# Splitting one block's weights early and turning two blocks on TensorE in an attention and expert kernel

## The chip, the cores and the metric

The program runs on one NeuronCore of a Trainium2 chip. The metric is the device time of one execution in microseconds (us); lower is better. The engines are named as in the profile: PE (TensorE matmuls; PEld its weight loads), DVE (VectorE), ACT (ScalarE), POOL (GpSimd) and SP (SyncE, which issues DMAs here). Each runs its own list of instructions in order and waits on semaphores of the others.

## What is computed

The kernel does a linear attention for 8 batches of 8 heads, 576 positions and 64 dimensions, and feeds each position's 512 values to one of 8 experts.

```python
q_s = exp(q - max(q)); q_s /= sum(q_s) + 1e-9        # over the 64 dimensions
k_s = exp(k - max(k)); k_s /= sum(k_s) + 1e-9        # over the 576 positions
kv  = einsum('bhsd,bhse->bhde', k_s, v)
x   = einsum('bhsd,bhde->bhse', q_s, kv)             # to (batch, position, 512)
logits = x @ w_gate; local_gate = sigmoid(x @ w_local)
for each position: e = argmax(logits), or the expert of the position before where local_gate >= 0.5
    h   = max(x @ w1[e], 0)                          # 512 -> 1024
    out = softmax(logits)[e] * (h @ w2[e])           # 1024 -> 512
```

## The kernel before

The first 200 us or so make the attention and write its rows to DRAM. The positions are then sorted by expert into blocks of 128 rows of one expert, numbered from 0; the tenth block is block 9 (`NP`, `NA` are 9). Blocks 0 to 8 are made from the first two of four row tiles while the attention of the rest still runs; their work stands in a list written out by hand, `ORDER`, in which a name such as `F1.8.0` is a task, its block and its half. `SWAP` names the tasks that run on their other engine (`alt` in `add`). From block 9 on a function `block(b)` writes the code of each block, and a nest of branches ends where no block is left.

The steps of a block are these; f counts the eight pieces of 128 columns of the hidden layer, 0 to 3 in half 0 and 4 to 7 in half 1:

- `G` gathers the block's rows (POOL's indirect DMA), `Px` scales them, `Ph` and `Pl` make a high and a low fp16 part (`x2`). The rows then have to be turned into `xT`: by a transposing DMA on SP (`D`, L880), or by eight PE transposes of 128x128 into the one PSUM tile `pt` (`T`, L874) and a DVE copy (`Tc`, L877).
- `F1.b.g` is the first product of a half (L903, L906; 48 matmuls), `Ar` and `Al` its ReLU as high and low part (ACT L911, DVE L915), `F2.b.g` the second product (L926; 12 matmuls), `Gv` the scaling of the result (ACT L929, which needs the share gathered by `Gp`) and `Pt` the scatter of the rows to the output (POOL L933).
- `RN.b.k` renews the weights where the block is the first of an expert, behind a branch on the flag in `info`: ACT cuts the high part (L190) and DVE the low part (L955) of four pieces. RN.b.0 holds w1's pieces 0 to 3, RN.b.1 its pieces 4 to 7, both out of the staging tile s1; RN.b.2 and RN.b.3 hold w2's out of s2. F1.b.0 needs RN.b.0, F1.b.1 needs RN.b.1.
- `s1.b` and `s2.b` (`fetch`, L998) load the next expert's w1 or w2 (2 MB each) into the staging tiles on SP, with a condition that skips the transfer; they wait until the tile has been cut. In `block(b)` these loads go in four quarters of 512 KB.
- In `hidden` PE uses 64 or 128 columns. From block 9 on PE reads a word of `info` for that (L838, once a block) and branches on it (L889, in both halves), over the code of the other form.
- `Sd.1` stores the shares of the second two tiles (SP); `Gp.9` gathers from them.

`Plan.emit` holds each list to its dependences; engines otherwise follow the written order. DMAs on SP are issued in order, and one that waits holds back those behind it.

Of the kernel before, what the change touches and what calls it, by code (L numbers as in the profile page):

```python
# [18 lines left out]
B, H, S, D = 8, 8, 576, 64  # L19
# [12 lines left out]
NA = 9  # L32
NB = NBM - NA
NP = NA
# [19 lines left out]
class Plan:  # L54
# [7 lines left out]
    def add(self, name, eng, fn, after=(), takes=(), uses=(), order=(), alt=None):  # L62


        eng = alt if name in self.swap else eng
        before = list(order) + list(uses)
        for r, _ in takes:
            if r in self.chained:
                before += [self.head[r]] if r in self.head else []
                self.head[r] = name  # L70
        self.tasks[name] = (eng, fn, list(after), list(takes), before, alt)
        for u in takes:
            self.taker[u] = name
        for u in set(uses) | set(takes):
            self.users.setdefault(u, []).append(name)
# [29 lines left out]


SWAP = """
Ph.0 Ph.11 Ph.2 Ph.3 Ph.4 Ph.6 Ph.9 Pl.10 Pl.11 Pl.6 Pl.8 Px.0 Px.10 Px.4 Px.5 Px.6 Px.9 Wh.15 ex.1.2 ex.3.0 ex.3.2 gs.0.0 gs.0.1 gs.0.2 gs.1.0 gs.1.1
gs.2.0 gs.2.1 gs.2.2 gs.3.0 gs.3.2 norm.3 norm.5 norm.6 put.0 put.2 put.3 put.4 put.6 put.7 qs.2.4 qs.3.6 qs.3.7 ro.0.0 ro.0.2 ro.0.3 ro.0.5 ro.0.7
ro.0.8 ro.1.3 ro.1.7 ro.2.0 ro.2.1 ro.2.2 ro.2.4 ro.2.6 ro.3.0 ro.3.4 ro.3.6 sub.6.1 vc.0.0 vc.0.1 vc.1.0 vc.2.0 vc.3.0 vc.4.0 vc.4.1 vc.5.0 xc.0.0  # L110
xc.0.2 xc.3.5 xc.3.8
# [35 lines left out]
ro.3.4 Ar.6.0 Al.6.0 ro.3.3 F2.5.1 ro.3.5 Sa.1 ro.2.0 Gv.5 RN.7.0 s2.5 RN.6.2 F1.6.1 Ar.6.1 ro.2.2 RN.7.1 RN.6.3 F2.6.0 F1.7.0 bo.3 D.8  # L147
Al.6.1 ro.3.6 s2.6 F2.6.1 ro.3.1 s1.7 RN.8.0 ro.2.1 Gv.6 Ar.7.0 RN.7.3 RN.7.2 bo.0 ro.3.2 bm.3 ro.2.7 Al.7.0 bm.1 bm.2 bm.0 bx.p0 bx
Sb.1 F1.7.1 Pt.5 Ar.7.1 Sc.1 Al.7.1 F2.7.0 F1.8.0 F2.7.1 s2.7 G.9 RN.8.2 Px.9 Ph.9 G.10 G.11 Pt.6 RN.8.1 s1.8 RN.8.3 s2.8
Px.10 Pl.9 Ar.8.0 Al.8.0 Gv.7 Px.11 F1.8.1 T.9 Tc.9 RN.9.1 Ar.8.1 Ph.10 Pt.7 Pl.10 D.10 G.12 F2.8.0 Gp.8 RN.9.0 Ph.11 Sd.1 Pl.11 Gp.9  # L150
Al.8.1 s1.9 D.11
"""


# [1 line left out]
def moe_kernel(ctx, tc, q, k, v, w_gate, w_local, w1, w2, out, dbg=None):  # L156
# [23 lines left out]
    def at(pair, b):  # L180

        return pair[0][:, b] if b < NA else pair[1][:, b - NA]
# [687 lines left out]
    def turn(b):  # L870

        for c in range(4):
            for i in range(2):
                nc.tensor.transpose(pt[0][:, i, c, :], x2[b % 2][:, i, P * c:P * c + P], id16)  # L874

    def turn_copy(b):
        nc.vector.tensor_copy(out=xT[b % 4], in_=pt[0])  # L877
# [5 lines left out]
    def ffn1(b, g):  # L883
        if b < NA:
            hidden(b, g, P)
            return
        if g == 0:
            few[0] = word(at(info, b)[:, 5:6], 1, [ET.PE])
        with tc.If(few[0] == 1) as cmp:  # L889
            hidden(b, g, P // 2)  # L890
        with cmp.Else():
            hidden(b, g, P)
# [77 lines left out]
    def renew(b, pieces):  # L970
        with tc.If(fst[b] == 1):  # L971
            for i in pieces:
                cut_hi(i, nc.scalar)
                cut_lo(i, nc.vector)
# [6 lines left out]
    def fetch(b, i, parts=None):  # L981

        if b >= NBM - 1:
            return
        w_ = at(info, b)
        cond, e = w_[:, 4:5], w_[:, 1:2]
        if NX0 <= b < NA:
            cond, e = w_[:, 2:3] if b == NX0 else w_[:, 0:1], w_[:, 3:4]
        if b not in due:
            due[b] = word(cond, 1, [ET.SP]), word(e, NE - 1, [ET.SP])  # L990
        cond, e = due[b]
        for n in ((None,) if parts is None else parts):
            s_, src = ((W["s1"], w1_src), (W["s2"], w2_src))[i - 1]
            s_, src = s_[:], src(bass.ds(e, 1))
            if n is not None:
                at_ = (slice(None), slice(None), slice(256 * n, 256 * n + 256)) if i == 1 else (slice(None), slice(2 * n, 2 * n + 2))
                s_, src = s_[at_], src[at_]
            nc.sync.dma_start(out=s_, in_=src, cond=(cond == 1), cond_hint=False)  # L998
# [4 lines left out]
    add, split = pl.add, pl.split  # L1003
    plan.append(pl)
    PE, DVE, ACT, POOL, SP = "PE", "DVE", "ACT", "Pool", "SP"
# [88 lines left out]
    for b in range(NP + 4):  # L1094
        add(("G", b), POOL, gather, after=[("ax",) if b < NA else ("bx",)] + [("xs", t, u) for t in range(2 if b < NA else NTILE) for u in range(3)],
            order=[("ow",)], takes=[("xg", b)])
        if b <= NP:
            add(("Gp", b), POOL, gather_share, after=[("ax",) if b < NA else ("bx",)] + [("Sd", t) for t in range(1 if b < NA else 2)],
                order=[("ow",)], takes=[("pb", b)])
        if b >= NP + 3:  # L1100
            continue
        add(("Px", b), POOL, prep_x, alt=DVE, after=[("G", b)], uses=[("xg", b)], takes=[("xn", b)])
        add(("Ph", b), ACT, prep_hi, alt=DVE, after=[("Px", b)], uses=[("xn", b)], takes=[("x2", b)])
        add(("Pl", b), DVE, prep_lo, alt=POOL, after=[("Ph", b)], uses=[("xn", b), ("x2", b)])
        if b in (0, NA):
            add(("T", b), PE, turn, after=[("Pl", b)], takes=[("pst", b)], uses=[("x2", b)])
            add(("Tc", b), DVE, turn_copy, after=[("T", b)], uses=[("pst", b)], takes=[("xT", b)])
        else:
            add(("D", b), SP, turn_dma, after=[("Pl", b)], uses=[("x2", b)], takes=[("xT", b)])
        if b > NP:  # L1110
            continue
        if b > 0:
            for i in range(2 if b == NP else 4):
                src = [("F1", b - 1, 0), ("F1", b - 1, 1), ("F2", b - 1, 0), ("F2", b - 1, 1)][i]
                add(("RN", b, i), ACT, renew4, after=[src, ("aj",) if b < NA else ("bj",)], order=[("s1" if i < 2 else "s2", b - 1)])
            add(("s1", b), SP, lambda b: fetch(b, 1), after=[("RN", b, 0), ("RN", b, 1)] + ([("bj",)] if b >= NX0 else []))
        else:
            add(("s1", b), SP, lambda b: fetch(b, 1), after=[("Wl", i) for i in range(8)] + [("aj",)], order=[("W", 3)])
        if b == NP:
            continue  # L1120
        add(("s2", b), SP, lambda b: fetch(b, 2),
            after=([("RN", b, 2), ("RN", b, 3)] if b else [("Wl", i) for i in range(8, 16)] + [("aj",)]) + ([("bj",)] if b >= NX0 else []))
        for g in range(2):
            wp_ = [("Wl", 4 * g + i) for i in range(4)] if b == 0 else [("RN", b, g)]
            add(("F1", b, g), PE, ffn1, after=[("Tc" if b in (0, NA) else "D", b)] + wp_, order=[("ow",)] + ([("F2", b - 1, g)] if b else [("F1", 0, 0)] * g)
                + ([("F1", b, 0)] if g else []), takes=[("psh", (b, g))], uses=[("xT", b)])
            add(("Ar", b, g), ACT, act_hi, after=[("F1", b, g)], uses=[("psh", (b, g))] + ([("hh", b)] if g else []), takes=[] if g else [("hh", b)])
            add(("Al", b, g), DVE, act_lo, after=[("Ar", b, g)], uses=[("psh", (b, g)), ("hh", b)])
            if b == NP - 1 and g:
                continue  # L1130
            wp_ = [("Wl", 8 + 4 * g + i) for i in range(4)] if b == 0 else [("RN", b, 2 + g)]
            add(("F2", b, g), PE, ffn2, after=[("Al", b, g)] + wp_, order=[("F1", b, 1)] if g == 0 else [("F1", b + 1, 0)],
                takes=[] if g else [("psy", b)], uses=[("hh", b)] + ([("psy", b)] if g else []))
        if b < NP - 1:
            add(("Gv", b), ACT, give, after=[("F2", b, 1), ("Gp", b)], uses=[("psy", b), ("pb", b)], takes=[("y", b)])
            add(("Pt", b), POOL, put, after=[("Gv", b)], uses=[("y", b)])
# [11 lines left out]
    def act(b, g):  # L1148
        act_hi(b, g)
        act_lo(b, g)  # L1150
# [5 lines left out]
    def block(b):  # L1156


        if b + AHEAD < NBM:
            gather(b + AHEAD)  # L1160
        prep_a(b + 3)
        if b + 1 < NBM:
            gather_share(b + 1)
            if b + 1 not in fst:
                flag(b + 1)
        ffn1(b, 0)
        act(b, 0)
        renew(b, FROM[b][0])
        fetch(b, 2, (0, 1) if b == NP else (1,))
        next_(b, (0, 1))  # L1170
        fetch(b + 1, 1, (0,))
        ffn2(b - 1, 1)
        ffn1(b, 1)
        give(b - 1)
        put(b - 1)
        renew(b, FROM[b][1])
        fetch(b, 2, (2,))
        next_(b, (2, 3))
        fetch(b + 1, 1, (1,))
# [64 lines left out]
```

## Time and profile before

| | before |
|---|---|
| median of 3 runs | 551.49 us (549.43 to 553.74) |
| profiled execution, its own time | 551.45 us |
| its span, first to last instruction | 549.7 us |
| PE busy | 493.6 us (90% of the span) |
| DVE, ACT, POOL busy | 276.2, 220.7, 258.1 us |
| mean granted clock of PE | 0.969 |

Times in the trace are counted from the span's start. A "busy" time of PE is modelled, so what counts are its gaps and their releasers: the instruction whose semaphore came last. "issue" stands for a wait with no releaser in the profile. The granted clock is a share of 2.4 GHz: 1.00 is that level, 0.50 is 1.2 GHz. A queue's "q" behind an engine's name (PEldq, SPq) marks instructions of its sequencer: loads of words, branches, issues of DMAs.

### The profile page before, as it was taken

The numbers are of one execution on the slowest core, as the hardware profiler recorded it, in microseconds if no ns is written. First come the engines' busy times: TensorE is split into PE (matmuls) and PEld (weight loads), VectorE is DVE, ScalarE is ACT, GpSimd is POOL, SyncE is SP. The second block draws the span as 40 slices with busy tenths as digits, with TensorE's granted clock in tenths as the row PEclk, the third lists the DMA queues.
The fourth block names the chain that finished last, engine by engine and source line by source line (L and its number), as shares of the span: only waits on it lengthen the run. The fifth ranks groups of instructions, "written<-read, shape, count | busy, mean of one in ns | idle before, by whom it ended". The sixth has DMA issues, their size and how long they took to land. (4 is left out here: it accounts for less than half of the span.)

```text
span 549.7 us, 19358 instructions
## 1 busy us (share of the span) xinstructions
PE 493.6 (90%) x7298; PEld 366.2 (67%) x7298; DVE 276.2 (50%) x501; ACT 220.7 (40%) x388; POOL 258.1 (47%) x284
## 2 busy tenths in 40 slices
PE   1657896767999999988999999999999999999994
PEld 0546775556776767666666777767677767767762
DVE  6889798897754672473128323822562122222221
ACT  1446587896321333343138223622642122222221
POOL 3666786356725340485425425424534324424431
PEclk9998797996999999989999999999999999999998
DMA  8999799487341449459538844872695233342342
GB/s 312 375 382 311 258 341 390 154 320 229 94 100 64 125 146 327 152 166 268 125 84 209 260 80 121 271 160 81 158 292 109 77 83 84 85 83 74 96 73 63
DMA packets 84351, 98.70 MB, mean 180 GB/s; under 512 B 46959, under 2 KB 61295, under 8 KB 84208
## 3 DMA queue, kind: packets, MB, share of 16 engines
q1 hardware_dynamic: 76560, 74.66, 48.0%
q0 software_dynamic: 7648, 22.20, 12.7%
q8 instruction: 82, 1.34, 1.0%
q14 instruction: 61, 0.50, 0.4%
HBM read 207.28 MB, written 20.89 MB: 415 GB/s over the span
## 5 line engine op out<-in xcount | busy, mean ns | idle before, releaser
L903 PE MATMUL ph<-xT,w1h 128*128 128x128 f16 (+1 forms) x2432 | 181.0, 218 | 0.5 <-issue 0.5
L903 PEld LDWEIGHTS <-w1h 128*128 128x128 f16 x2432 | 145.4, 98 | 0.7 <-issue 0.6
L915 DVE SCALAR_TENSOR_TENSOR lo<-ph,hi 128x512 f16<-128x512 f32 x76 | 52.3, 688 | 138.7 <-ACTq L971 130.9
L933 POOL DMA_INDIRECT out<-y,sidx x38 | 40.1, 1056 | 173.3 <-ACTq L971 145.4
L906 PE MATMUL ph<-xT,w1l 128*128 128x128 f16 (+1 forms) x1216 | 115.8, 218 | 5.4 <-issue 2.8
L911 ACT ACTIVATE hi<-ph 128x512 f16<-128x512 f32 x76 | 45.2, 595 | 181.5 <-PE ph L903 124.3
L906 PEld LDWEIGHTS <-w1l 128*128 128x128 f16 x1216 | 82.1, 98 | 23.5 <-issue 4.0
L926 PEld LDWEIGHTS <-hi 128*128 128x128 f16 x608 | 56.2, 98 | 54.4 <-issue 0.2
L926 PE MATMUL py<-w2h,hi 128*128 128x512 f16 x184 | 70.0, 381 | 0.0
L926 PE MATMUL py<-w2l,hi 128*128 128x512 f16 x184 | 69.8, 380 | 0.0
L926 PE MATMUL py<-w2h,lo 128*128 128x512 f16 x184 | 69.7, 379 | 0.0
L867 DVE SCALAR_TENSOR_TENSOR x<-xn,x 128x512 f16<-128x512 f32 x37 | 31.6, 853 | 69.1 <-ACT x L190 65.2
L844 POOL DMA_INDIRECT xg<-xrows,gidx x42 | 46.5, 1106 | 23.8 <-DVE tz L679 12.1
L926 PEld LDWEIGHTS <-lo 128*128 128x128 f16 x304 | 29.8, 98 | 36.0 <-issue 0.3
L926 PE MATMUL pi<-w2h,hi 128*128 128x512 f16 x120 | 45.5, 379 | 0.0
L926 PE MATMUL pi<-w2l,hi 128*128 128x512 f16 x120 | 45.5, 379 | 0.0
L926 PE MATMUL pi<-w2h,lo 128*128 128x512 f16 x120 | 45.5, 379 | 0.0
L850 POOL DMA_INDIRECT pb<-shares,gidx x39 | 41.5, 1065 | 8.3 <-issue 8.2
L431 POOL TENSOR_TENSOR qs<-qt,qm 128x512 f32<-128x512 f32 x33 | 35.3, 1082 | 18.9 <-PE pq L440 17.1
L855 POOL TENSOR_TENSOR xn<-xg 128x512 f32<-128x512 f32 x35 | 37.1, 1060 | 10.9 <-DMA xg<-xrows,gidx 5.0
L322 DVE TENSOR_REDUCE KM<-KT 128x128 f32<-128x1152 f32 x16 | 34.6, 2172 | 4.3 <-DMA KT<-in_k 4.3
L455 PE MATMUL px<-R,qe 64*64 64x74 f32 x864 | 23.2, 249 | 12.3 <-ACT xt L190 6.5
(219 smaller groups left out, 585.0 us busy)
## 6 DMA issues: line engine op xcount, KB each, us to landing
s<-in_moe_w SPq DMA_DIRECT2D x233, 512.0 KB
s<-in_moe_w SPq DMA_DIRECT2D x19, 2048.0 KB
xrows<-xt SPq DMA_DIRECT2D x12, 888.0 KB
KT<-in_k SPq DMA_DIRECT2D x16, 576.0 KB
VT<-in_v SPq DMA_DIRECT2D x16, 576.0 KB
qt<-in_q SPq DMA_DIRECT2D x8, 640.0 KB
qt<-in_q SPq DMA_DIRECT2D x8, 512.0 KB
s<-in_moe_w SPq DMA_DIRECT2D x4, 1024.0 KB
```

The costliest lines, as they stand in the source:

```text
L322: nc.vector.tensor_reduce(out=KM[b % 2][:, 2 * u:2 * u + 2], in_=KT[b % NKT][:, u:KG:2].rearrange("p g c d -> p g d c"), axis=AX.X, op=ALU ...
L431: on("qs", t, c).tensor_tensor(out=qs[t, c].rearrange("p (g x) d -> p g x d", x=2), in0=qt[t, u][:, :, i, :].rearrange("p (x g) d -> p g x ...
L844: nc.gpsimd.indirect_dma_start(out=xg[b % AHEAD], out_offset=None, in_=src, in_offset=bass.IndirectOffsetOnAxis(ap=i_[:, j_:j_ + 1], axis=0))
L850: nc.gpsimd.indirect_dma_start(out=pb[b % NPB], out_offset=None, in_=src, in_offset=bass.IndirectOffsetOnAxis(ap=i_[:, j_:j_ + 1], axis=0))
L855: eng.tensor_tensor(out=xn[b % 2].rearrange("p (g x d) -> p g x d", g=4, x=2), in0=xg[b % AHEAD].rearrange("p (g x) -> p g x", g=4)[:, :, ...
L867: nc.vector.scalar_tensor_tensor(out=x2[b % 2][:, 1, :], in0=xn[b % 2], scalar=XS, in1=x2[b % 2][:, 0, :], op0=ALU.mult, op1=ALU.subtract)
L903: nc.tensor.matmul(ph_[:, f, 0:n], W["w1h"][:, c, fs], xT_[:, i, c, 0:n], start=False, stop=(c == 3 and i == 1))
L906: nc.tensor.matmul(ph_[:, f, 0:n], W["w1l"][:, c, fs], xT_[:, 0, c, 0:n], start=(c == 0), stop=False)
L911: nc.scalar.activation(hi[b % 2][:, 4 * g:4 * g + 4, :], phs[g], AF.Relu)
L915: nc.vector.scalar_tensor_tensor(out=lo[b % 2][:, gs_, :], in0=phs[g], scalar=0.0, in1=hi[b % 2][:, gs_, :], op0=ALU.max, op1=ALU.subtract)
L926: nc.tensor.matmul(result(b), h_[:, f, :], w_[:, f, :], start=(f == 0 and i == 0), stop=(f == 7 and i == 2))
L933: nc.gpsimd.indirect_dma_start(out=outr, out_offset=bass.IndirectOffsetOnAxis(ap=i_[:, j_:j_ + 1], axis=0), in_=ys[b % 2], in_offset=None, ...
```

## The change

The change reorders the end of `ORDER`, from the tenth block's weights on, and touches the planner and `block`:

- RN.9.0 stands right behind Al.8.0, ahead of Gv.7 and of F1.8.1 (it stood last among block 9's cuts, behind Ar.8.1 and Ph.10).
- Blocks 10 and 11 (the eleventh and twelfth) are turned by PE as block 9 is: T.10 and Tc.10 in `ORDER`, block 11's turn in `block(9)`. Their transposing DMAs D.10 and D.11 are gone.
- Pl.10 and Pl.11 leave `SWAP`: they run on DVE, no longer as two instructions each on POOL.
- The load s1.9 is issued as s1.9.0 and s1.9.1, two quarters each, behind RN.9.0 and behind RN.9.1; it was one DMA of 2 MB behind both.

```diff
-Ph.0 Ph.11 Ph.2 Ph.3 Ph.4 Ph.6 Ph.9 Pl.10 Pl.11 Pl.6 Pl.8 Px.0 ...
+Ph.0 Ph.11 Ph.2 Ph.3 Ph.4 Ph.6 Ph.9 Pl.6 Pl.8 Px.0 ...
...
-Px.10 Pl.9 Ar.8.0 Al.8.0 Gv.7 Px.11 F1.8.1 T.9 Tc.9 RN.9.1 Ar.8.1 Ph.10 Pt.7 Pl.10 D.10 G.12 F2.8.0 Gp.8 RN.9.0 Ph.11 Sd.1 Pl.11 Gp.9
-Al.8.1 s1.9 D.11
+Px.10 Pl.9 Ar.8.0 Al.8.0 RN.9.0 Gv.7 Px.11 Ph.10 Pl.10 F1.8.1 T.9 RN.9.1 Tc.9 Sd.1 s1.9.0 s1.9.1 G.12 Ar.8.1 Al.8.1 F2.8.0 T.10 Tc.10 Pt.7 Ph.11 Pl.11
+Gp.8 Gp.9
...
-        if b in (0, NA):
+        if b == NP + 2:
+            continue
+        if b in (0, NP, NP + 1):
             add(("T", b), PE, turn, after=[("Pl", b)], takes=[("pst", b)], uses=[("x2", b)])
...
+            if b == NP:
+                for i in range(2):
+                    add(("s1", b, i), SP, lambda b, i: fetch(b, 1, (2 * i, 2 * i + 1)), after=[("RN", b, i), ("bj",)])
+                continue
...
         ffn1(b, 0)
+        if b == NP:
+            turn(b + 2)
         act(b, 0)
+        if b == NP:
+            turn_copy(b + 2)
         renew(b, FROM[b][0])
```

On PE, between the end of F2.8.0 and the start of F1.9.0, there stands before:

```order
L926 LDWEIGHTS lo_1975
L926 MATMUL py_1966<-w2h,lo_1975 128x512
L838 TENSOR_LOAD info_78
L889 COMPARE_AND_BRANCH
L906 LDWEIGHTS w1l
L906 MATMUL ph_1979<-xT_1958,w1l 128x64
```

and with the change, where the last of T.10's eight transposes are the first rows (x_1955 is block 10's x2, pt_1965 the one PSUM tile for transposes):

```order
L874 LDWEIGHTS x_1955
L874 MATMUL pt_1965<-id_67,x_1955 128x128
L838 TENSOR_LOAD info_78
L889 COMPARE_AND_BRANCH
L906 LDWEIGHTS w1l
L906 MATMUL ph_1979<-xT_1958,w1l 128x64
```

The word's load and the branch, which followed F2.8.0 directly, now follow T.10, whose first transpose has to wait for Pl.10 and for Tc.9. The eight transposes of T.11 stand in the same way between F1.9.0 and F2.8.1.

On DVE, from Al.8.0 to Al.8.1, there stands before (x4 are the four cuts of an RN, first RN.9.1, then RN.9.0; xT_1958 is block 9's, L194 is Ph.11):

```order
L915 SCALAR_TENSOR_TENSOR lo_1975<-ph_1979,hi_1973 128x512
L877 COPY xT_1958<-pt_1965 128x1024
L838 TENSOR_LOAD info_78
L971 COMPARE_AND_BRANCH
L955 SCALAR_TENSOR_TENSOR w1l<-s_1934,w1h 128x4x128 x4
L971 UNCONDITIONAL_BRANCH x2
L971 COMPARE_AND_BRANCH
L955 SCALAR_TENSOR_TENSOR w1l<-s_1934,w1h 128x4x128 x4
L971 UNCONDITIONAL_BRANCH x2
L194 TENSOR_SCALAR x_1956<-xn_1954 128x512
L915 SCALAR_TENSOR_TENSOR lo_1975<-ph_1980,hi_1973 128x512
```

and with the change (the first x4 is RN.9.0, the second RN.9.1, the L867 row is Pl.10, xT_1959 is block 10's):

```order
L838 TENSOR_LOAD info_78
L971 COMPARE_AND_BRANCH
L955 SCALAR_TENSOR_TENSOR w1l<-s_1934,w1h 128x4x128 x4
L971 UNCONDITIONAL_BRANCH x2
L867 SCALAR_TENSOR_TENSOR x_1955<-xn_1953,x_1955 128x512
L971 COMPARE_AND_BRANCH
L955 SCALAR_TENSOR_TENSOR w1l<-s_1934,w1h 128x4x128 x4
L971 UNCONDITIONAL_BRANCH x2
L877 COPY xT_1958<-pt_1965 128x1024
L915 SCALAR_TENSOR_TENSOR lo_1975<-ph_1980,hi_1973 128x512
L889 UNCONDITIONAL_BRANCH
L877 COPY xT_1959<-pt_1965 128x1024
```

Tc.9, which came before all eight cuts, comes behind them, and Pl.10 stands between the two fours.

On SP, the issues behind the load s2.8 stand before as:

```order
L880 DMA_TRANSPOSE xT_1959<-x_1955 128x8x128
L583 DMA shares<-pr 128x2x9
L838 TENSOR_LOAD info_78 x2
L998 REGISTER_ALU x2
L998 ISA
L998 DMA s_1934<-in_moe_w 128x4x1024
L889 UNCONDITIONAL_BRANCH
L880 DMA_TRANSPOSE xT_1960<-x_1956 128x8x128
```

and with the change as:

```order
L583 DMA shares<-pr 128x2x9
L971 UNCONDITIONAL_BRANCH
L838 TENSOR_LOAD info_78 x2
L998 REGISTER_ALU x2
L998 ISA
L998 DMA s_1934<-in_moe_w 128x4x256
L998 ISA
L998 REGISTER_ALU
L998 ISA
L998 DMA s_1934<-in_moe_w 128x4x256
```

Two more quarters like the last follow. The two transposing DMAs around the share store and the load are gone, and the store is first.

## Rows read from the trace of the kernel before

**Rows 1.** Page: busy us (share of the span), instructions.
```profile
PE 493.6 (90%) x7298; PEld 366.2 (67%) x7298; DVE 276.2 (50%) x501; ACT 220.7 (40%) x388; POOL 258.1 (47%) x284
```

**Rows 2.** Stretches: length, then PE, PEld, DVE, ACT, POOL busy, clock, DMA share, GB/s.
```profile
235.07:237.68 2.61, 0.00 (x1) 0.00 (x1) 2.61 (x4) 0.93 (x2) 2.37 (x3) 1.00 0.00 0
...
238.90:242.30 3.40, 3.40 (x32) 3.09 (x30) 1.47 (x3) 0.37 (x1) 3.29 (x3) 0.50 0.77 148
242.30:255.30 13.00, 13.00 (x132) 8.59 (x129) 7.80 (x12) 6.77 (x13) 8.43 (x8) 1.00 1.07 240
255.30:256.77 1.47, 0.00 (x1) 0.00 (x1) 0.00 (x0) 0.99 (x2) 1.31 (x2) 1.00 1.08 398
...
262.22:262.71 0.49, 0.00 (x0) 0.00 (x0) 0.00 (x0) 0.00 (x0) 0.35 (x1) 1.00 0.14 42
262.71:542.40 279.69, 279.69 (x3252) 201.57 (x3252) 91.08 (x129) 92.95 (x156) 111.82 (x106) 1.00 0.52 129
```

**Rows 3.** Waits of PE from 205 us on: us in total, times, longest.
```profile
PE ph L906 <- DVE w1l L955: 2.6, 1, 2.6
```

**Rows 4.** Stretches as in rows 2: F1.8.1; F2.7.1 and F1.8.1; F1.9.0 and F2.8.1.
```profile
229.19:231.87 2.68, 2.68 (x49) 2.68 (x48) 0.00 (x0) 1.94 (x4) 1.01 (x1) 1.00 0.03 9
...
226.60:231.87 5.27, 5.27 (x63) 3.84 (x61) 1.33 (x3) 2.54 (x5) 2.05 (x2) 1.00 0.05 16
237.68:244.60 6.92, 6.92 (x60) 5.29 (x61) 4.73 (x9) 2.67 (x5) 6.04 (x6) 0.75 0.75 167
```

**Rows 5.** ACT in order of time: start us, us, instruction, idle before and its releaser.
```profile
226.80 0.60 ACT L911 ACTIVATE hi<-ph 128x512 f16<-128x512 f32 x1 [5.62 <-PE ph L903]
229.39 0.69 ACT L929 ACTIVATE y<-py,pb 128x512 f32<-128x512 f32 x1 [1.99 <-PE py L926]
230.30 1.15 ACT L190 ACTIVATE w1h<-s 128x512 f16<-128x512 f32 x2 [0.22 <-ACT y L929]
...
233.82 2.18 ACT L190 ACTIVATE w1h<-s 128x512 f16<-128x512 f32 x4
```

**Rows 6.** DVE in order of time; then the eight cuts by line (ns min/median/max).
```profile
232.52 0.69 DVE L877 COPY xT<-pt 128x1024 f16<-128x1024 f16 x1 [4.40 <-PE pt L874]
233.16 6.28 DVE L955 SCALAR_TENSOR_TENSOR w1l<-s,w1h 128x512 f16<-128x512 f32 x8
...
L955 DVE SCALAR_TENSOR_TENSOR w1l<-s,w1h x8: 676/682/1634, 233.2 to 238.8; 128x512 f16<-128x512 f32 x8
```

**Rows 7.** POOL in order of time: the two instructions of Pl.10.
```profile
234.01 1.80 POOL L864 TENSOR_SCALAR xn<-xn 128x512 f32<-128x512 f32 x1 [2.63 <-ACT x L190]
235.89 1.19 POOL L865 TENSOR_TENSOR x<-xn,x 128x512 f16<-128x512 f32 x1
```

**Rows 8.** PE's branches at L889: count, ns min/median/max, first and last start.
```profile
L889 PEldq COMPARE_BRANCH  x1: 4476/4476/4476, 252.2 to 252.2; - x1
...
L889 PEldq COMPARE_BRANCH  x1: 2902/2902/2902, 259.8 to 259.8; - x1
...
L889 PEldq COMPARE_BRANCH  x59: 63/210/1117, 265.1 to 536.6; - x59
```

**Rows 9.** DMA queues from 242.3 to 254.2 us: packets, MB, share of 16 engines.
```profile
q1 hardware_dynamic: 1608, 2.42, 90.6%
...
q14 instruction: 1, 0.01, 0.2%
```

**Rows 10.** SP in order of time: the w1 load (one DMA) and D.11.
```profile
240.41 0.38 SPq L998 DMA_DIRECT2D s<-in_moe_w  x1
243.08 4.06 SPq L880 DMA_TRANSPOSE xT<-x  x1
```

**Rows 11.** PE in order of time at T.9; then PE's word loads by line (ns).
```profile
231.87 0.61 PE L874 MATMUL pt<-id,x 128*128 128x128 f16 x8
232.32 0.38 PE L926 MATMUL py<-w2h,hi 128*128 128x512 f16 x1
...
L838 PEldq TENSOR_LOAD <-info x7: 299/313/774, 232.1 to 299.4; - x7
```

More of the change, by code (lines that the diff above doesn't have):

```diff
@@ L107 @@
 SWAP = """
-Ph.0 Ph.11 Ph.2 Ph.3 Ph.4 Ph.6 Ph.9 Pl.10 Pl.11 Pl.6 Pl.8 Px.0 Px.10 Px.4 Px.5 Px.6 Px.9 Wh.15 ex.1.2 ex.3.0 ex.3.2 gs.0.0 gs.0.1 gs.0.2 gs.1.0 gs.1.1
+Ph.0 Ph.11 Ph.2 Ph.3 Ph.4 Ph.6 Ph.9 Pl.6 Pl.8 Px.0 Px.10 Px.4 Px.5 Px.6 Px.9 Wh.15 ex.1.2 ex.3.0 ex.3.2 gs.0.0 gs.0.1 gs.0.2 gs.1.0 gs.1.1
 gs.2.0 gs.2.1 gs.2.2 gs.3.0 gs.3.2 norm.3 norm.5 norm.6 put.0 put.2 put.3 put.4 put.6 put.7 qs.2.4 qs.3.6 qs.3.7 ro.0.0 ro.0.2 ro.0.3 ro.0.5 ro.0.7
@@ L1124, in moe_kernel @@
             wp_ = [("Wl", 4 * g + i) for i in range(4)] if b == 0 else [("RN", b, g)]
-            add(("F1", b, g), PE, ffn1, after=[("Tc" if b in (0, NA) else "D", b)] + wp_, order=[("ow",)] + ([("F2", b - 1, g)] if b else [("F1", 0, 0)] * g)
+            add(("F1", b, g), PE, ffn1, after=[("Tc" if b == 0 else "D", b)] + wp_, order=[("ow",)] + ([("F2", b - 1, g)] if b else [("F1", 0, 0)] * g)
                 + ([("F1", b, 0)] if g else []), takes=[("psh", (b, g))], uses=[("xT", b)])
```

## The prediction

> **What bounds the kernel now.** I read the page's busy table first: PE works 90% of the span [rows 1], so the question is where it does not. The table by stretches splits the second half at PE's gaps [rows 2]. From 262.71 to 542.4 us PE is busy 279.69 of 279.69 us at granted clock 1.00: whatever is saved before 262.71 reaches the end unchanged, because nothing behind it waits for a clock of its own. Three gaps stand ahead of it: 2.61 us, 1.47 us and 0.49 us. Between the first two lies a stretch of 3.40 us in which the granted clock is 0.50, the lower of its two levels, after the longest gap; behind the gaps of 1.47 and 0.49 it stayed at 1.00.
>
> The first gap has a named releaser, the vector engine's split of w1 [rows 3]: PE has finished F2.8.0 (first half of block 8's second product) and F1.9.0 may not begin before the w1 of block 9 is cut. The chain behind it reads: ACT cuts f-pieces 4 to 7 first, from 230.30, and pieces 0 to 3, which F1.9.0 needs, from 233.82 [rows 5]; DVE follows with eight cuts from 233.16 in 6.28 us [rows 6], though F1.8.0, the last reader of pieces 0 to 3, had been over at 226.6 (its release of ACT at 226.80 is in [rows 5]). Two of the eight took up to 1.63 us against a middle value of 0.68 [rows 6], while POOL ran Pl.10 in 1.80 and 1.19 us [rows 7].
>
> The price of the slow clock: a second-product half and a first-product half (F2.7.1, F1.8.1) take 5.27 us together, 2.68 of it the first product; F1.9.0 and F2.8.1 took 6.92 [rows 4]. That is 1.65 us.
>
> The other two gaps have no releaser in the waits; what ends at the same time is PE's branch at L889, which picks the 64- or 128-column form. It took 4.48 us from 252.2 (to 256.7; PE resumes at 256.77) and 2.90 us from 259.8 (to 262.7); the 59 behind have a middle of 0.21 and a maximum of 1.12 [rows 8]. Between 242.3 and 254.2 no packet of the code queue q8 ran, while q1 held 90.6% of the engines' time [rows 9]: the 2 MB w1 load issued at 240.41 and, queued behind it, the transposing DMA of 243.08 [rows 10]. I read both gaps as code that came late behind that traffic.
>
> **The change, part by part.**
>
> *RN.9.0 (pieces 0 to 3) moves ahead of Gv.7.* On ACT it follows Ar.8.0. From y (229.39) to the first cut (230.30) the flag load and branch cost 0.91, so the first cut comes at 226.80 + 0.91 = 227.7 and the four end near 227.7 + 2.18 = 229.9 [rows 5]. DVE, idle until 232.52, starts one cut behind (228.3) and needs 4 x 0.68, until about 231. Nobody pays: Gv.7 slips some 0.4 us to 229.9, its result is read out before F2.8.0 writes the same PSUM at 232.32 [rows 11]; the put of block 7 slips behind it and behind the gather G.12 by about 1 us, with nothing waiting. Without that cover the slip would be PE's.
>
> *Pl.10 and Pl.11 go from POOL (3.0 us each, [rows 7]) to DVE at about 0.69 (as the copy's 0.69, [rows 6]).* Pl.10 waits for Ph.10 (ACT: 229.9 + 0.69 for Gv.7 + some 0.6 = 231.2) and ends near 231.9. RN.9.1 follows ACT, whose last cut now ends near 231.2 + 2.2 = 233.4, so DVE ends near 234.1; POOL has no arithmetic there, so I take 0.68 per cut and not 1.63. Then Tc.9: 0.69, ready at 234.8. The bound from the other side: two of the four cuts at 1.63, as many slow ones as the eight of before had, give 236.7.
>
> *T.10 stands between F2.8.0 and F1.9.0.* F2.8.0 ends at 235.07 [rows 2]. T.10 needs the one PSUM tile pt free (Tc.9, 234.8) and then costs 232.32 - 231.87 = 0.45 us [rows 11]: 235.5. Behind it stand the load of the block's word and the branch. Before, these ran at 232.1, hidden under F2.8.0; now PE's queue can't run ahead past T.10's wait. They take 0.30 to 0.77 and about 0.21 [rows 8, 11], partly under T.10. F1.9.0 starts between 235.5 (all hidden) and 238.0 (Tc.9 at 236.7, T.10, then load and branch in full); I take 236.2, the middle load of 0.31 and a branch of 0.21 with the gaps between them and nothing of it hidden, since that load is the usual one and Tc.9 at 234.8 the nearer case. **Start: 237.68 - 236.2 = 1.5 us gained** (bounds: 2.2 gained, 0.3 lost).
>
> *The clock.* The remaining idle time comes in pieces of under 0.8 us; a whole 1.47 us left the clock at 1.00 [rows 2]. **1.65 us gained** (bounds 0 and 1.65).
>
> *T.11 between F1.9.0 and F2.8.1* costs **0.45 us** of PE. Its input Pl.11 ends near 237.4 and Tc.10 near 236.4; F1.9.0 ends at 238.9, so neither is waited for. Tc.10 and Tc.11 add 0.69 each to DVE, which is busy 7.80 of 13.00 us in the stretch behind [rows 2]; if that cover were gone, 1.4 us of w2 cuts would come late for the second product.
>
> *SP.* D.10, D.11 vanish; the w1 load leaves in four quarters, two after RN.9.0 (about 231), two after RN.9.1 (about 234.2), 6 to 9 us earlier than the 240.41 of [rows 10]. Its 2 MB should so be through about as much earlier, ahead of the stretch in which no code came [rows 9]. Its reader, the first block of the next expert, is blocks away. The share store Sd.1 no longer waits behind D.10, and Gp.9 with it. D.12, the next transposing DMA, meets only w2 quarters. **1.47 + 0.49 = 1.96 us gained** if the two late branches go (bounds: 1.96 and 0).
>
> Sum: -1.5 - 1.65 + 0.45 - 1.96 = **-4.7 us**. The profiled execution took 551.45 us (span 549.7), as good as the median 551.49: **546.8 us**.
>
> A rule that speaks against the last term: the Trainium skill, "Runtime: NRT & Kernel Launch", section "Instruction fetch mechanics", says that a taken branch whose target isn't in the pages held forces a fetch before execution goes on. By it the stalls hang on where the code lies, not on traffic; the sum would be -2.7. The trace agrees that a branch waited, but 59 like it behind did not; the result is the first rival below.
>
> **The rivals.**
> - *The late code stays late* (or another branch gets it: PE's code before F1.10.0 grows by 32 instructions, so pages begin elsewhere). For it: the 4.48 us branch began where the w1 load was already over. Against: 59 later branches at most 1.12 [rows 8]. 551.45 - 2.7 = 548.8.
> - *The branch behind T.10 gets it.* That one has lost its cover: one wait like the 4.48 us of [rows 8] puts F1.9.0 at 235.5 + 0.4 + 4.5 = 240.4, 2.7 later than before, with the slow clock kept: +2.7 + 0.45 - 1.96 = +1.2, **552.6, slower**; with the old gaps kept 554.6. It decides from a start of F1.9.0 later than 237.68 + 1.96 - 0.45 = 239.2. For it: the place is new and bare. Against: the middle branch takes 0.21 [rows 8], and only the first w1 quarters run ahead of this one.
> - *DVE stays the bound*: Tc.9 now queues behind RN.9.1, the wait is exchanged for one on pt. F1.9.0 at 238.0, clock slow: +0.3 + 0.45 - 1.96 = -1.2, 550.2. For it: 1.63 us cuts happened [rows 6]. Against: their partner on POOL is gone.
> - *The clock falls all the same*: 546.8 + 1.65 = 548.4.
>
> **How the numbers follow.** Forecast 0.50, late code stays 0.27, bare branch 0.08, DVE 0.08, clock 0.07. Around the forecast the start's bound gives down to 546.1; the runs before spread from 549.43 to 553.74, about 2 us to each side, which takes the low end to 544. The high end, 551, holds the second, fourth and fifth case with part of that spread and leaves out the bare branch. One per cent, about what a measurement of this kernel can tell, is 5.5 us, or 546.0 downwards: only the lower third of the forecast's case, and little of the others, comes out there: faster 0.24. Slower by 1% would be 557, beyond even the bare branch: 0.04. The rest, 0.72, is within 1%.
>
> **What would show it.** In the changed profile PE's gap ahead of F1.9.0 should be under 0.8 us with releaser issue or the copy of pt, no longer the w1 cut; F1.9.0 should last 2.68 us at clock 1.00; w1 cuts at L955 should come in two groups of four from 228.4 and 231.8, none near 1.6 us; sixteen more transposes at L874 cost 0.9 us; the longest L889 branch should be near 1.1 us and PE without a gap from block 10 on. The forecast is wrong if a branch over 3 us remains, if DVE's copy at L877 ends after 235.5, or if the granted clock falls between 236 and 246.

## The result, and the profile after

The changed kernel takes 546.41 us (median of 22 runs, 544.38 to 550.28) where the kernel before takes 552.11 on the same chips (22 runs, 548.61 to 556.26): a ratio of 0.9897, 95% interval 0.9872 to 0.9922, 5.7 us less. Forecast were 546.8 and 4.7 less. Measured twice more beside other kernels the ratio was 0.9857 (0.9821 to 0.9893) and 0.9897 (0.9851 to 0.9943).

PE's busy share and count on the page, as [rows 1], and its waits from 205 us to the end, as [rows 3] (us in total, times, longest):

```profile
PE 494.1 (91%) x7314; PEld 367.2 (68%) x7314; DVE 278.2 (51%) x505; ACT 220.8 (41%) x388; POOL 253.6 (47%) x280
```

```profile
PE ph L906 <- issue: 0.4, 1, 0.4
PE ph L903 <- issue: 0.4, 1, 0.4
```

The wait for DVE's w1 cut (2.6 us) is gone. Before, PE also waited three times for issue at L906:

```profile
PE ph L906 <- issue: 2.8, 3, 1.5
```

Two of these, 1.47 and 0.49 us [rows 2], stood ahead of the late branches' matmuls and are gone. The third, 0.79 us, lay inside F1.8.0, ahead of the change, as the 0.4 us at L903 does now. The 0.4 us at L906 is new: it is the bare branch ahead of F1.9.0. Stretches of the changed kernel, as [rows 2] (length, then busy of PE, PEld, DVE, ACT, POOL, the granted clock, DMA share, GB/s):

```profile
234.99:235.41 0.42, 0.01 (x2) 0.01 (x1) 0.38 (x1) 0.00 (x0) 0.42 (x1) 1.00 1.04 397
235.41:238.10 2.69, 2.69 (x49) 2.69 (x49) 2.57 (x3) 0.00 (x0) 2.52 (x3) 1.00 1.04 344
238.10:241.13 3.03, 3.03 (x23) 1.62 (x21) 1.97 (x4) 2.59 (x5) 0.04 (x1) 1.00 0.70 222
241.13:262.21 21.08, 21.08 (x241) 15.42 (x240) 8.72 (x13) 7.18 (x13) 9.07 (x8) 1.00 0.66 183
262.21:536.78 274.57, 274.57 (x3193) 197.76 (x3191) 89.20 (x128) 92.52 (x155) 112.75 (x105) 1.00 0.50 128
```

In order: the gap ahead of F1.9.0, F1.9.0, T.11 with F2.8.1, and then everything to the last matmul without a gap, all of it at granted clock 1.00. PE's branches at L889 over the whole run, as [rows 8] (count, ns min/median/max):

```profile
L889 PEldq COMPARE_BRANCH  x64: 63/212/891, 235.1 to 530.9; - x64
```

The two of 4.48 and 2.90 us have no successor. ACT, DVE and PE in order of time, as [rows 5, 6, 11] (start us, us, instruction, idle before and its releaser):

```profile
226.18 0.60 ACT L911 ACTIVATE hi<-ph 128x512 f16<-128x512 f32 x1 [5.20 <-PE ph L903]
226.68 2.19 ACT L190 ACTIVATE w1h<-s 128x512 f16<-128x512 f32 x4
```

```profile
227.75 2.97 DVE L955 SCALAR_TENSOR_TENSOR w1l<-s,w1h 128x512 f16<-128x512 f32 x4
230.65 0.68 DVE L867 SCALAR_TENSOR_TENSOR x<-xn,x 128x512 f16<-128x512 f32 x1
231.25 2.48 DVE L955 SCALAR_TENSOR_TENSOR w1l<-s,w1h 128x512 f16<-128x512 f32 x4
233.66 0.68 DVE L877 COPY xT<-pt 128x1024 f16<-128x1024 f16 x1
...
235.64 1.65 DVE L194 TENSOR_SCALAR x<-xn 128x512 f16<-128x512 f32 x1
```

```profile
234.39 0.61 PE L874 MATMUL pt<-id,x 128*128 128x128 f16 x8
235.41 0.40 PE L906 MATMUL ph<-xT,w1l 128*128 128x128 f16 x4 [0.41 <-issue]
```

RN.9.0 comes straight behind Ar.8.0, its flag load hidden; its cuts are done at 230.7, Pl.10 takes 0.68 on DVE, and Tc.9 ends at 234.34, when T.10 may start. The word's load and the branch behind T.10 leave PE 0.41 us without work (from T.10's start to that of F1.9.0 it is 1.02 us, where T.9 took 0.45: a price of 0.57).

**A ruler for the experiments.** How early block 8 is reached differs by up to 6.7 us between profiled executions (F2.7.1 starts at 221.88 in one, at 228.56 in another), in code that no kernel here changes. So the kernels are compared below by a stretch of PE's own time line, from the start of F2.7.1 to that of F1.12.0, in three parts: A to F1.9.0 (the wait), B to F1.9.1 (the clock, one turn), C to F1.12.0 (late code). In the kernel before it runs from 226.60 [rows 4] to 273.26. Each kernel was profiled once, the changed one three times; C comes out at 26.35 in all seven profiles that have neither late code nor a turn in it. Medians and ratios are of the timed runs; kernels of one group shared a chip and their runs of the kernel before.

| kernel | A | B | C | stretch, us | median, us | ratio to before (95%) |
|---|---|---|---|---|---|---|
| before | 11.08 | 6.92 | 28.66 | 46.66 | | |
| changed | 9.43 | 5.73 | 26.35 | 41.50 | 546.41 | 0.9897 (0.9872 to 0.9922) |
| e1_early | 8.31 | 5.27 | 31.41 | 44.98 | 546.13 | 0.9944 (0.9907 to 0.9982) |
| e2_whole | 9.93 | 5.73 | 26.35 | 42.01 | 543.29 | 0.9887 (0.9828 to 0.9945) |
| e3_dma | 9.07 | 5.27 | 30.42 | 44.74 | 548.01 | 1.0024 (0.9986 to 1.0061) |
| e4_pool | 10.92 | 6.53 | 26.35 | 43.80 | 546.67 | 0.9939 (0.9906 to 0.9972) |
| after2 (changed) | 9.92 | 5.73 | 26.35 | 41.99 | 542.55 | 0.9857 (0.9821 to 0.9893) |
| e5_both | 10.12 | 5.73 | 28.65 | 44.50 | 546.98 | 0.9955 (0.9929 to 0.9981) |
| e6_plain | 9.17 | 5.27 | 26.35 | 40.79 | 543.66 | 0.9872 (0.9832 to 0.9913) |
| e7_turns | 11.09 | 7.35 | 26.80 | 45.24 | 546.58 | 0.9953 (0.9924 to 0.9983) |
| after3 (changed) | 10.26 | 5.73 | 26.35 | 42.33 | 542.94 | 0.9897 (0.9851 to 0.9943) |
| best2 | 8.31 | 5.72 | 26.80 | 40.82 | 542.38 | 0.9885 (0.9833 to 0.9936) |
| e8_one | 8.31 | 5.72 | 26.78 | 40.81 | 541.16 | 0.9864 (0.9817 to 0.9912) |
| e9_noload | 9.23 | 5.73 | 26.35 | 41.31 | 546.84 | 0.9826 (0.9719 to 0.9934) |

A ratio goes with its interval and compares fast runs alone, while the medians are of all runs, so it need not be the quotient of two medians (e3, e9). The medians of before were 549.54 for e1 to e4, 549.11 for after2 to e7, 549.92 for after3, best2 and e8, 553.30 for e9.

### The profile page after: what moved, and what is told of

Its sections match the earlier page's. It is cut to its first block, busy times and chain, and to the rows that moved or that the text cites. A ratio compares the mean times of both kernels' runs of the same rounds, so it can differ in the third digit from the quotient of the medians.

```text
span 543.4 us, 19390 instructions
## 1 busy us (share of the span) xinstructions
PE 494.1 (91%) x7314; PEld 367.2 (68%) x7314; DVE 278.2 (51%) x505; ACT 220.8 (41%) x388; POOL 253.6 (47%) x280
## 5 line engine op out<-in xcount | busy, mean ns | idle before, releaser
L903 PE MATMUL ph<-xT,w1h 128*128 128x128 f16 (+1 forms) x2432 | 179.9, 217 | 0.4 <-issue 0.4
L903 PEld LDWEIGHTS <-w1h 128*128 128x128 f16 x2432 | 144.3, 98 | 1.3 <-issue 1.3
L906 PE MATMUL ph<-xT,w1l 128*128 128x128 f16 (+1 forms) x1216 | 115.4, 217 | 0.9 <-issue 0.9
L906 PEld LDWEIGHTS <-w1l 128*128 128x128 f16 x1216 | 81.7, 98 | 17.6 <-issue 0.7
L867 DVE SCALAR_TENSOR_TENSOR x<-xn,x 128x512 f16<-128x512 f32 x39 | 31.7, 812 | 71.5 <-ACT x L190 70.6
L844 POOL DMA_INDIRECT xg<-xrows,gidx x42 | 48.9, 1163 | 23.8 <-DVE tz L679 12.1
L855 POOL TENSOR_TENSOR xn<-xg 128x512 f32<-128x512 f32 x35 | 37.1, 1062 | 9.0 <-DVEq L971 3.2
L455 PE MATMUL px<-R,qe 64*64 64x74 f32 x864 | 24.5, 256 | 13.2 <-ACT xt L190 6.1
```

The lines of the kernel that those rows point to most:

```text
L844: nc.gpsimd.indirect_dma_start(out=xg[b % AHEAD], out_offset=None, in_=src, in_offset=bass.IndirectOffsetOnAxis(ap=i_[:, j_:j_ + 1], axis=0))
L855: eng.tensor_tensor(out=xn[b % 2].rearrange("p (g x d) -> p g x d", g=4, x=2), in0=xg[b % AHEAD].rearrange("p (g x) -> p g x", g=4)[:, :, ...
L867: nc.vector.scalar_tensor_tensor(out=x2[b % 2][:, 1, :], in0=xn[b % 2], scalar=XS, in1=x2[b % 2][:, 0, :], op0=ALU.mult, op1=ALU.subtract)
L903: nc.tensor.matmul(ph_[:, f, 0:n], W["w1h"][:, c, fs], xT_[:, i, c, 0:n], start=False, stop=(c == 3 and i == 1))
L906: nc.tensor.matmul(ph_[:, f, 0:n], W["w1l"][:, c, fs], xT_[:, 0, c, 0:n], start=(c == 0), stop=False)
```

## The experiments

**e1_early: one part alone, the early cuts.**

```diff
-Px.10 Pl.9 Ar.8.0 Al.8.0 Gv.7 Px.11 ... Gp.8 RN.9.0 Ph.11 Sd.1
+Px.10 Pl.9 Ar.8.0 Al.8.0 RN.9.0 Gv.7 Px.11 ... Gp.8 Ph.11 Sd.1
```

> The kernel before with one edit: RN.9.0 stands right behind Al.8.0. The turns stay transposing DMAs, Pl.10 and Pl.11 stay on POOL, the w1 load stays one DMA. Both theories: F1.9.0 follows F2.8.0 with no gap over 0.3 us (start about 235.1), lasts 2.68 us, and no clock of 0.50 from 235 to 246; that is 2.6 + 1.65 = 4.2 us less than before. They part on the late code. Traffic (my theory: code comes late behind the one 2 MB w1 load and the transposing DMA): both are still there, only some 2 to 4 us earlier, so PE still has 1.5 to 2.5 us of gaps between 240 and 265 with branches at L889 of over 2 us; time before minus 4.2, ratio 0.992. Rival (the position of the load in time alone decides, not its shape): no gap, time before minus 6.4, ratio 0.988.

F1.9.0 follows F2.8.0 without a gap, and lasts 2.68 us: A and B fall by 2.77 and 1.65, as both theories had it. The late code stays, and is worse: one branch of 5.44 us ends in a gap of 2.85 us, and the clock falls behind that one instead. The gap, and the two stretches that are F1.11.0:

```profile
253.17:256.02 2.85, 0.00 (x0) 0.00 (x1) 1.03 (x2) 1.11 (x2) 2.03 (x2) 0.90 1.05 394
256.02:257.40 1.38, 1.38 (x14) 1.38 (x15) 0.26 (x1) 0.00 (x0) 0.26 (x1) 0.50 1.04 385
257.40:260.04 2.64, 2.64 (x38) 2.64 (x36) 0.00 (x0) 0.00 (x0) 2.31 (x3) 0.73 1.51 250
```

The profile names a DVE instruction of a later block's rows (x L867) as this gap's releaser, which F1.11.0 does not read; the branch ended at 255.96, 0.06 us ahead of the first matmul, as the two of before did. Of 4.42 us gained ahead, C takes 2.75 back. The rival, the load's place in time, is not tested here: by the ruler the load left no earlier (14.2 us behind the start of F2.7.1, 13.8 before), and the transposing DMAs lay within 0.4 us of their old places, while PE reached this code 4.4 us earlier. e3 and e5 below have the earlier load.

**e2_whole: the w1 load in one piece again.**

```diff
-Tc.9 Sd.1 s1.9.0 s1.9.1 G.12
+Tc.9 Sd.1 s1.9 G.12
```

> The changed kernel with block 9's w1 load as one DMA of 2 MB behind RN.9.1 (about 235), everything else as changed; PE's code is the same instruction for instruction. Traffic, if the one large DMA is the cause: PE gaps of 1.5 to 2.5 us come back between 240 and 265 with a branch at L889 over 2 us, ratio to before 0.994. Traffic, if the transposing DMAs behind the load are the cause: no gap, 0.990. Layout (the stalls hang on where PE's code lies): no gap, 0.990.

No late code reaches PE: C is 26.35 as in the changed kernel, though the 2 MB left as one DMA. Two branches took 1.32 and 1.38 us, both under a running product. The quarters bring nothing that this ruler sees, and the large load is not the cause by itself.

**e3_dma: transposing DMAs again, all else as changed.**

```diff
-Al.8.1 F2.8.0 T.10 Tc.10 Pt.7 Ph.11 Pl.11
+Al.8.1 F2.8.0 D.10 Pt.7 Ph.11 Pl.11 D.11
...
-        if b == NP:
-            turn(b + 2)
```

> The changed kernel with blocks 10 and 11 turned by transposing DMAs again (D.10 behind F2.8.0, D.11 last); Pl.10 and Pl.11 on DVE, RN.9.0 early and the quartered load stay. PE loses 16 transposes (0.9 us) and the branch ahead of F1.9.0 is covered again (0.4 us). Traffic by transposing DMAs, or layout (PE's code is that of the kernel before): late branches come back, 1.5 to 2.5 us of PE gaps between 240 and 265, ratio to before 0.992. Large load alone the cause: no such gap, 1.3 us less than the changed kernel, ratio 0.987.

C is 30.42, 4.1 us over the changed kernel's. One gap of 3.8 us stands ahead of F1.10.0; the branch there took 5.89 us, and D.10 itself, issued at 233.54, released the first matmul. PE's waits:

```profile
PE ph L906 <- DMA xT<-x: 3.8, 1, 3.8
PE ph L906 <- DVE xT L877: 0.6, 1, 0.6
```

So the quarters don't protect the code, nor does a load that leaves 5 to 9 us earlier by the ruler (4.3 to 8.6 us behind the start of F2.7.1). Here the late rows and the late code can't be told apart, nor transfers from the layout of PE's code, which is that of the kernel before. That took e5 and e6. The timed runs show no gain over before (1.0024, where 0.992 was expected), though the stretch is 1.9 us shorter; where the rest goes is open.

**after2: the changed kernel beside them.**

> The changed kernel once more, so that the three beside it can be compared with it on the same chip. Every theory: no PE gap over 0.5 us from block 10 on, F1.9.0 at clock 1.00, ratio to before 0.990.

A is 9.92, for a wait of 0.42 us ahead of T.10 for Tc.9 that the first profile does not have; B and C are the same.

**e5_both: the two DMAs added, PE's code untouched.**

```diff
-Al.8.1 F2.8.0 T.10 Tc.10 Pt.7 Ph.11 Pl.11
+Al.8.1 F2.8.0 T.10 D.10 Tc.10 Pt.7 Ph.11 Pl.11 D.11
...
+    def turn_spare(b):
+        nc.sync.dma_start(out=spare[b % 2]..., in_=x2[b % 2]..., transpose=True)
```

> The changed kernel with the two transposing DMAs D.10 and D.11 added again, into a spare tile that nothing reads; PE's instructions stay those of the changed kernel one for one, and nothing waits for the two transfers. Theory now (the transposing DMAs hold back the code, as the runs with them against those without suggest): PE gaps of 1.5 to 4 us at a branch of L889 come back between 238 and 262, ratio to before 0.993 to 0.997. Rival (the place of PE's code in its pages decides, 32 instructions more or fewer): no gap over 0.5 us, ratio 0.990.

The gaps come back, 0.99 and 0.92 us, ended by branches of 3.16 and 3.50 us, though nothing reads what the two DMAs bring:

```profile
251.31:252.30 0.99, 0.00 (x1) 0.00 (x1) 0.00 (x0) 0.69 (x1) 0.00 (x0) 1.00 1.03 380
252.30:257.74 5.44, 5.44 (x60) 3.76 (x60) 1.39 (x2) 1.23 (x2) 4.12 (x4) 1.00 1.12 256
257.74:258.66 0.92, 0.01 (x2) 0.01 (x1) 0.00 (x0) 0.00 (x0) 0.00 (x0) 1.00 0.10 30
```

PE's branches at L889, which is L895 in this kernel:

```profile
L895 PEldq COMPARE_BRANCH  x1: 3156/3156/3156, 249.1 to 249.1; - x1
...
L895 PEldq COMPARE_BRANCH  x1: 3502/3502/3502, 255.1 to 255.1; - x1
```

C is 28.65, that of the kernel before (28.66), and the median 4.4 us above after2's. With PE's instructions the same one for one, the layout of its code is out as the cause of these.

That these branches wait for code, the packets of the code queue q8 show. All profiles together have twelve branches of over 1.2 us in this stretch (two each before and in e2, e5 and e8, one in e1, three in e3), and each ends 1.3 to 1.5 us behind the end of a 16 KB packet of q8. The two packets of e5 took 1.14 and 1.03 us, as others do, but started late: 9.2 and 15.5 us behind the start of F1.9.1, where the changed kernel, with the same code on PE, has its two at 3.4 to 6.0 and 10.1 to 10.8 us in its three profiles.

**e6_plain: the same bytes without the turn.**

```diff
+    def plain(b):
+        nc.sync.dma_start(out=xT[b % 4]..., in_=x2[b % 2]...)
...
-            add(("D", b), SP, turn_dma, after=[("Pl", b)], ...)
+            add(("D", b), SP, plain if b > NP else turn_dma, after=[("Pl", b)], ...)
```

> The kernel of e3_dma with D.10 and D.11 as plain copies of the same 256 KB, without the turn, so that the rows of blocks 10 and 11 are not turned and their products are left meaningless; PE's instructions are those of the kernel before. Theory now (the transposing form is what holds the code back): no PE gap over 0.6 us from 238 to 265, 3.5 us less than e3_dma, ratio to before 0.988. Rival (place of PE's code): the gap of over 2 us at a branch stays, ratio 0.995 to 1.000.

No late code: C is 26.35 with PE's instructions of the kernel before. It is the transposing form. Packets and the hardware queue q1 from 233 to 248 us, first of e5_both, then of e6_plain:

```profile
DMA packets 4238, 3.21 MB, mean 214 GB/s; under 512 B 2294, under 2 KB 3886, under 8 KB 4236
...
q1 hardware_dynamic: 3975, 2.60, 91.4%
```

```profile
DMA packets 3359, 4.91 MB, mean 327 GB/s; under 512 B 280, under 2 KB 2264, under 8 KB 3356
...
q1 hardware_dynamic: 2951, 3.75, 77.4%
```

The two transposing DMAs are some 2,000 packets of under 512 B; with them the queue fills the engines' time while it moves less.

**e7_turns: the other part alone, the turns on PE.** RN.9.0 late, one load of 2 MB, Pl on POOL.

```diff
-Pl.10 D.10 G.12 ... Al.8.1 s1.9 D.11
+Pl.10 G.12 ... Al.8.1 s1.9
...
         ffn1(b, 0)
+        if b == NP:
+            turn(b + 1)
...
         ffn1(b, 1)
+        if b == NP:
+            turn(b + 2)
```

> The kernel before with one part of the change: blocks 10 and 11 turned by PE (behind F1.9.0 and behind F1.9.1, two places at which no branch loses its cover), D.10 and D.11 gone; RN.9.0 stays late, Pl.10 and Pl.11 on POOL, the w1 load one DMA of 2 MB. Theory now: the gap of about 2.6 us ahead of F1.9.0 and the slow clock behind it stay, the late branches of before go (2.3 us), the turns cost 0.9: ratio to before 0.997. Rival (the large load holds the code): late branches stay, ratio 1.002.

The late code is gone (C: 26.35 and 0.45 for the turn of block 11) with a load that left 13.0 us behind the start of F2.7.1, 0.8 us earlier than before; the wait and the slow clock are as before:

```profile
230.35:232.97 2.62, 0.00 (x1) 0.00 (x1) 2.62 (x4) 0.76 (x2) 2.38 (x3) 1.00 0.00 0
232.97:237.14 4.17, 4.17 (x48) 4.17 (x49) 2.69 (x5) 0.00 (x0) 3.79 (x3) 0.63 0.50 109
```

**e9_noload: e5_both without the w1 load.**

```diff
-Tc.9 Sd.1 s1.9.0 s1.9.1 G.12
+Tc.9 Sd.1 G.12
```

> The kernel of e5_both without the w1 load of block 9: its four quarters (2 MB) are left out, so that the next expert's first product is made with old weights. D.10 and D.11 still run into the spare tile. If it takes the load beside the transposing DMAs to hold the code back: no PE gap over 0.3 us at a branch, the stretch from the start of F2.7.1 to that of F1.12.0 lasts 41.5 to 42.3 us as in the changed kernel (44.5 in e5_both), time 2 to 3 us below e5_both's. If the transposing DMAs do it alone: gaps of about 0.9 us stay, 44 to 44.5 us.

No late code: the longest branch is 0.43 us and C is 26.35, with both transposing DMAs there. The same window of 233 to 248 us:

```profile
DMA packets 2765, 2.04 MB, mean 136 GB/s; under 512 B 2272, under 2 KB 2272, under 8 KB 2761
...
q1 hardware_dynamic: 2433, 1.15, 38.5%
```

It takes both, the load and the transposing DMAs: the same small packets, with q1 at 38.5% of the engines' time in place of 91.4%, delay nothing. The stretch is 3.2 us shorter than e5_both's; the timed runs, four of them, agree with that only roughly (ratio 0.9826 beside 0.9955).

**e4_pool: Pl.10 and Pl.11 back on POOL.**

```diff
-Ph.9 Pl.6 Pl.8
+Ph.9 Pl.10 Pl.11 Pl.6 Pl.8
```

> The changed kernel with Pl.10 and Pl.11 back on POOL. My theory (two POOL instructions of 1.80 and 1.19 us slow DVE's cuts): one or two of RN.9.1's four cuts take 1.1 to 1.6 us instead of 0.62, Tc.9 ends at 235 to 236 instead of 234.3, F1.9.0 starts 0.7 to 1.7 us later than 235.4, with the clock still 1.00; ratio to before 0.991 to 0.993. Rival (the cuts and the POOL work don't meet, or the slack ahead of T.10 holds them): F1.9.0 within 0.3 us of 235.4, ratio 0.990.

The stretch is 1.5 to 2.3 us longer than in the changed kernel's three profiles, in A and in B; part of it, the second wait, I had not expected. PE's waits, and DVE's eight cuts by line (ns min/median/max):

```profile
PE pt L874 <- DVE xT L877: 1.4, 1, 1.4
PE pt L874 <- POOL x L865: 0.6, 1, 0.6
PE ph L906 <- issue: 0.4, 1, 0.4
```

```profile
L955 DVE SCALAR_TENSOR_TENSOR w1l<-s,w1h x8: 678/679/1641, 225.2 to 231.3; 128x512 f16<-128x512 f32 x8
```

Two cuts take 1.09 and 1.64 us beside POOL's two instructions, Tc.9 comes 1.43 us late, and T.11 waits for POOL's Pl.11. In the changed kernel the longest cut is 1.17 us, beside POOL's Px.11. In every profile a w1 cut that began under a tensor_tensor of POOL (Px, Pl) ended 0.55 us behind that instruction's end; the cuts of 1.64 and 1.17 us are of this kind. That Pl runs on DVE is worth 1.5 to 2.3 us of the stretch; it is no side effect.

**after3, best2, e8_one: what is left at F1.9.0, and a single transposing DMA.** best2 puts Tc.9 ahead of RN.9.1, T.10 behind F1.9.0 and T.11 behind F1.9.1; e8_one is best2 with block 11 by D.11.

```diff
-F1.8.1 T.9 RN.9.1 Tc.9 Sd.1 ... Al.8.1 F2.8.0 T.10 Tc.10 Pt.7
+F1.8.1 T.9 Tc.9 RN.9.1 Sd.1 ... Al.8.1 F2.8.0 Pt.7
...
         ffn1(b, 0)
         if b == NP:
-            turn(b + 2)
+            turn(b + 1)
...
         ffn1(b, 1)
+        if b == NP:
+            turn(b + 2)
```

> The changed kernel again, as the measure for the two beside it on the same chip. Every theory: a wait of 0 to 0.5 us ahead of T.10 for the copy Tc.9 and a gap of 0.4 us ahead of F1.9.0 with the releaser issue; ratio to before 0.986 to 0.990.

> The changed kernel with Tc.9 ahead of RN.9.1's cuts on DVE, T.10 behind F1.9.0 and T.11 behind F1.9.1, so that the word's load and the branch run under F2.8.0 again. My theory (0.41 us of bare branch and up to 0.42 us of wait for Tc.9 are all that is left there): no PE gap over 0.2 us between F2.7.1 and block 12, from the start of F2.7.1 to that of F1.11.0 30.5 us instead of 30.96 to 31.46; time 0.4 to 0.9 us below the changed kernel, ratio to before 0.985 to 0.989. Rival (the branch or the code's fetch shows elsewhere): the stretch stays at 31 us.

> The kernel of best2 with block 11 turned by a transposing DMA (D.11, the last of the list), block 10 by PE: one transposing DMA beside the w1 load where e3_dma had two. If it takes both of them to hold the code back: no PE gap over 0.5 us, 0.45 us less than best2. If one is enough: one late branch of 1 us or more between 240 and 262, 0.5 to 3 us more than best2.

after3 waits 0.76 us ahead of T.10 for Tc.9, longer than expected. In best2 PE has no gap at all in the whole stretch:

```profile
226.30:267.12 40.82, 40.82 (x460) 29.48 (x457) 23.37 (x36) 18.12 (x32) 21.97 (x20) 1.00 0.64 191
```

That is 0.7 to 1.5 us less than the three profiles of the changed kernel; the medians (542.38 beside 542.94) are too close to tell the two apart. e8_one has two long branches, one of 2.64 us under a running product and one of 2.86 us with a loss of 0.42 us in C, and saves a turn of 0.45: 40.81, even with best2. Its one transposing DMA costs far less than the two of e5 (2.3), so neither of its expectations fits quite. The number of them is not all: in the kernel before, the packets of D.10 (1,024 of 256 bytes) started between 238.3 and 239.7 us, ahead of the first of the load at 241.5, so that D.11 alone met the load there, and the late code cost 2.3 us. And in the changed kernel D.12, a transposing DMA issued at 249.24 between two quarters of a load, held nothing back (longest branch 0.89). What sets the price is open.

## Why the prediction was right, step by step

- **Start of F1.9.0, forecast 1.5 us gained.** A fell by 1.65 us in the first profile, by 1.16 and 0.82 in the two others; the forecast start of 236.2, with F2.7.1 at 226.60 [rows 4], is an A of 9.60, and it was 9.43, 9.92 and 10.26. The bare load and branch left PE idle for 0.41 or 0.42 us in all three. What varies is Tc.9, which I had ready 0.3 us ahead of T.10: it queues behind RN.9.1 on DVE and kept T.10 waiting for up to 0.76 us. I had DVE's cuts start when ACT's first one ends; they start when DVE's own list gets there. That list runs with hardly a pause from Px.9 (L855), which waits for its gathered rows, to Tc.9. Px.9 began 1.72, 1.22 and 0.89 us ahead of F2.7.1 in the three profiles, and that lead and A add up to 11.15 in each, to 0.01. The 0.91 us of a flag load and a branch on ACT is a misreading, 0.69 of it is Gv.7 itself: the first cut came 0.50 us behind the start of Ar.8.0. The late Tc.9 is the rival "DVE stays the bound" at a part of its price; best2 removes it by the order of two tasks.
- **Clock, 1.65 us.** F1.9.0 takes 2.69 us at 1.00. e1 shows the gain with the wait gone, e7 the loss with the wait kept.
- **T.11, 0.45 us lost.** B is 5.73 with it and 5.27 without (e3, e6).
- **Late code, 1.96 us gained.** That code came late behind the traffic holds (e5), the size was off: C fell by 2.31. I added up the idle of PE's rows; ends of matmuls are modelled there, and starts from one group to the next show 0.3 us more. The cause was put too broadly: I gave the credit to the load that leaves earlier and in quarters. e2 has no late code with the whole load, e3 and e5 have it with quarters that leave 5 to 9 us earlier. What the change does for the code is take D.10 and D.11 off, which the prediction names but gives no price; what they need to do harm is the load beside them (e9). With the load moved alone this term would have failed.
- **Code layout.** e5 has the changed kernel's instructions on PE and the stalls, e6 those of the kernel before and none, so where the code lies did not decide. The Trainium skill ("Runtime: NRT & Kernel Launch", section "Instruction fetch mechanics") has a taken branch outside the pages held wait for a fetch: the branches of 3 to 5 us agree with that, but taken as a forecast of the time, by which the stalls would follow the layout, the trace disagrees.
- **Sum.** In the stretch 4.7 us were forecast and 5.2, 4.7 and 4.3 measured; that it fits so well is in part luck, as the start gained up to 0.7 less than forecast and the late code 0.35 more. The profiled spans differ by 6.2 us (549.7 and 543.4): 5.2 in the stretch, 0.6 because F2.7.1 was reached earlier, and the rest almost all behind the last matmul. The last two lie where nothing was changed, and by the spread of F2.7.1 they are no part of the effect that one profile can show. In the other two groups the ratios make 7.9 and 5.7 us of some 549 us, so that 1.3 to 3.2 us of the timed gain lie outside the stretch there; in their profiles the part behind the stretch is 1.4 and 1.6 us shorter than in the one of before (275.1 and 274.9 beside 276.4), and why is open. The measured 1.0% lies at the line that the forecast drew between faster (0.24) and within 1% (0.72), with the interval on both sides of it.
- **The early cuts need the turns.** Ahead of C, e1 gains 4.42; in C, e7 gains 2.31; the two turns cost 0.9. That makes 5.8, and best2's stretch is 5.84 shorter than before. Yet alone e1 keeps 1.68 of it and e7 1.42: e1's gain is eaten by later code and a second fall of the clock, e7 pays for the turns.

## What to carry to other kernels

Where PE waits at a branch and no engine is late, look for transposing DMAs issued beside a large load: D.10 and D.11 cost 2.3 us here, the same turns on PE, itself the bound, 0.9. Move an instruction's cover with it: a word's load and a branch cost nothing under a running product and left PE idle for 0.41 us behind a wait. Where executions scatter by more than an edit is worth, measure it between two events on the bounding engine's own time line.

## What the chip did that I had not expected

- A long gap does not always bring the slow clock. In or behind gaps of 2.61 [rows 2], 2.62 (e7) and 2.85 us (e1) it fell to 0.50; in and behind the 3.79 us of e3 it did not:

```profile
244.34:248.13 3.79, 0.00 (x0) 0.10 (x1) 0.00 (x0) 0.00 (x0) 0.09 (x1) 1.00 1.26 80
248.13:250.81 2.68, 2.68 (x49) 2.68 (x48) 1.97 (x4) 2.15 (x4) 2.23 (x2) 1.00 1.07 409
```

  What tells it from the others is open.
- DVE's Ph.11 took 1.65 us in the changed kernel, beside POOL's Px.12 (235.92 to 236.99), and 0.42 in e4 with POOL idle beside it: moving Pl off POOL did not end all such meetings, it moved them to where nothing waits.
- How a transposing DMA beside a load delays a code packet, no view here shows: in e5 the last of their 256-byte packets started at 246.4 us, 3.3 us ahead of the first late code packet. That is open.
